# An attention and wave-MLP kernel: new shape of the k and v loads, new order of the first loads, turns by transfers in the last batches, and another planner

## The chip, the cores and the metric

The kernel runs on one core of a Trainium2 chip. The metric is the device time of one execution in microseconds. Five engines work side by side, each through its own list of instructions in order: TensorE (PE, matrix products; PEld is its loading of weights), VectorE (DVE), ScalarE (ACT), GpSimd (POOL) and SyncE (SP, which here only issues transfers). Transfers are issued by SP, ACT or POOL and carried by 16 DMA engines. An instruction that waits holds up all that stand behind it on its engine.

## What is computed

For each of 8 batches, with 576 rows, 8 heads of width 64, and C = 512:

```
kv    = k^T v                      per head (64 x 64)
x     = (q kv) / rms(q kv) * g     heads side by side: 576 x 512
theta = x w_theta
y     = w_tok_r (x cos theta) + w_tok_i (x sin theta)     mixes the 576 rows
u     = x + y
out   = u + max(u w_ch, 0)
```

Inputs are float32, the output is float32; products after kv are done in float16 with float32 sums. The order in which kv sums the 576 rows does not matter to the result beyond rounding.

## The kernel before

Each batch is cut into four full row tiles of 128 rows (tile j holds the rows 4p + j of the first 512) and one tail tile of 64 rows, which is folded into 128 partitions by 256 columns. A batch goes through these steps, whose names are those of the planner:

- load k and v (SP; in batch 0 v by ACT) and q (POOL, which turns float32 into float16 on the way). `load_heads` (L191 to L199) reads four rows per partition, 1 KB, and the 64 last rows as 256-byte pieces into partitions 0 to 63.
- `kv` (L250): 40 products per batch into PSUM; `ko`: copies into the block-diagonal `kbd`.
- q is turned (rows to columns): by PE and a copy in batches 0 and 1 (`qt`, `qo`), by a transposing transfer on SP from batch 2 on (`qd`, L300).
- `raw` (L313, L322): q kv. `sq` (ACT) squares, `ss` (DVE) sums, `rt` (POOL, L351) takes the root, `x` (DVE, L363) multiplies.
- `xt`, `xo`: PE turns x by four transposes a tile (L268) into the PSUM ring `tr` of two, ACT copies the result (L284).
- `th` (L393, L398): x w_theta. `pt` (ACT, L411) and `arg` (DVE, L417) take whole turns off, `abs` (DVE), `sin` (L433) and `cos` (L440) on ACT, `z` (DVE, L453) multiplies by x. The tail tile is moved by four transfers (`zmove`, L461) into `zt`.
- `y` (L476, L480): 9 products a full tile in three parts, with the token weights `wT`. `um` (DVE, L487) adds x. `ut`, `uo`: u is turned as x is. `v` (L393, L398; the same helper): u w_ch. `ug` (POOL, L516) scales u, `fin` (DVE, L526) joins, `st` (SP, L535, L540) stores.

The token weights are loaded once, by POOL, and turned by PE (`wt`, L565, L566: 50 transposes), the copies (`wo`) shared by ACT and DVE. w_theta (L608) lands in the third z buffer and is scaled by DVE (`wth`). w_ch (L611) lands in the buffer of the untransposed token weights, so that its load waits until they have been turned; ACT scales it (`wc`, L552).

The order of all this is not in loops. `add` makes a task for each step, with an engine, a cost and a place in the row; `in_order` (L65) then plays the engines against each other: among the tasks that could start first on an engine it takes the one with the smallest place plus an offset (`OFF`, by kind and phase), and the instructions are recorded in that order. Loads are tasks of a pretended engine "wire" that carries one after another at 3.9 us a megabyte (`MB`). Buffers are rings (`Ring`); `HOP`, `RESHAPE` and `STAY` are costs of going from engine to engine and of changing the shape of PE's products.

Two gates hold transfers back: POOL copies one element of the first v piece before it loads the second half of q, and SP moves one element of the token weights before it loads k and v of batch 1.

Of the kernel before, what the change touches and what calls it, by code (L numbers as in the profile page):

```python
# [17 lines left out]
def off(kind, phase):  # L18
    return OFF.get(kind, (0.0,) * 4)[phase]


# [7 lines left out]
class Task:  # L29


    def __init__(self, kind, eng, cost, fn, deps, pos, takes, tail, shape):
        self.kind, self.eng, self.cost, self.fn, self.deps = kind, eng, cost, fn, deps
        self.phase = 0 if pos < 5 else 1 if pos < 10 else 2 if pos < 35 else 3
        self.key, self.takes, self.tail, self.shape = pos + off(kind, self.phase), takes, tail, shape
        self.readers = []
        self.end = None

OFF = {
    "abs": (-3.7, 3.6, -2.4, -8.5), "arg": (6.9, 12.9, 14.0, 13.4),
    "cos": (13.4, 13.4, 8.2, 7.8), "fin": (14.6, 7.0, 14.8, 13.7),
    "g": (13.0, 13.0, 13.0, 13.0), "hold": (14.0, 14.0, 14.0, 14.0),
    "ko": (11.8, 8.0, 14.0, 13.9), "kv": (13.8, -0.2, 6.1, 7.1), "load": (-5.7, 1.3, 2.9, 2.9),
    "pt": (-7.8, 2.2, -7.1, 3.8), "qd": (11.0, 10.6, 4.6, 4.6), "qo": (-8.0, -2.1, -2.1, -2.1),
    "qt": (4.1, 6.8, 6.8, 6.8), "raw": (-1.7, -7.2, -6.3, -3.9), "rt": (-0.5, 3.8, -5.8, -4.4),
    "sin": (-0.9, 13.7, 7.2, 4.4), "sq": (-1.7, -6.0, -5.7, 1.0), "ss": (-0.6, 4.1, -7.7, 11.0),
    "st": (-7.1, -7.4, -6.6, -8.0), "th": (-1.4, -6.3, 0.6, -1.3),
    "ug": (13.0, 13.9, 12.5, 9.1), "um": (13.8, 13.7, 13.7, 11.8),  # L50
    "uo": (5.2, -4.0, -0.3, -0.7), "ut": (-7.1, 19.0, 15.2, 13.7), "v": (13.7, 12.7, 16.9, 7.7),
    "wc": (-8.0, -8.0, -8.0, -8.0), "wire": (-4.0, -4.8, -4.7, -4.7),
    "wo": (-5.3, -5.3, -5.3, -5.3), "wt": (-1.7, -1.7, -1.7, -1.7),
    "wth": (-4.7, -4.7, -4.7, -4.7), "x": (-8.9, -0.3, -6.7, 5.3),
    "xo": (-7.6, -1.6, -2.9, -1.3), "xt": (-4.2, 7.2, -4.8, 6.1), "y": (13.4, 13.6, 15.3, 14.4),
    "z": (7.4, 4.5, 7.3, 9.7), "zmove": (5.3, 11.7, 6.1, 12.8),
}
HOP = 0.14
SLACK = 0.000
RESHAPE = 0.1  # L60
HEAD = 0.0
STAY = 3.861


def in_order(tasks, spare=(), idle=None):  # L65

    waiting = list(tasks)
    free, shape, order = {}, {}, []  # L70
    while waiting:
        best = {}
        for t in waiting:
            if any(d.end is None for d in t.deps):
                continue
            at = free.get(t.eng, 0.0)
            for d in t.deps:
                at = max(at, d.end + (d.tail + HOP if d.eng != t.eng else 0.0))
            held = [r.held[len(r.held) - r.n] for r in t.takes if len(r.held) >= r.n]
            readers = [x for h in held for x in h.readers]  # L80
            if any(x.end is None for x in readers):
                continue
            for x in readers:
                at = max(at, x.end + (HOP if x.eng != t.eng else 0.0))
            turn = t.shape is not None and shape.get(t.eng, t.shape) != t.shape
            best.setdefault(t.eng, []).append((at, t.key + STAY * turn, t))
        if not best:
            raise ValueError("no task can start")
        picks = []
        for cand in best.values():  # L90
            first = min(c[0] for c in cand)
            picks.append(min(((key, at, i, t) for i, (at, key, t) in enumerate(cand)
                              if at <= first + SLACK), key=lambda c: c[:3]))
        _, at, _, t = min(picks, key=lambda c: (c[1], c[0]))
        was = free.get(t.eng, 0.0)
        n = int((at - was - 0.3) / 0.3) if t.eng == "PE" and was < HEAD else 0
        for r in spare:
            old = r.held[len(r.held) - r.n].readers if len(r.held) >= r.n else []
            if n > 1 and r not in t.takes and all(x.end is not None and x.end + HOP < was for x in old):
                d = Task("idle", "PE", 0.0, lambda r=r, n=n: idle(r, n), [], 0.0, [r], 0.0, None)  # L100
                d.end = was
                r.held.append(d)
                order.append(d)
                break
        t.end = at + t.cost
        if t.shape is not None:
            t.end += RESHAPE * (shape.get(t.eng, t.shape) != t.shape)
            shape[t.eng] = t.shape
        free[t.eng] = t.end
        for r in t.takes:  # L110
            r.held.append(t)
        waiting.remove(t)
        order.append(t)
    return order
# [3 lines left out]
def kernel(  # L118
# [36 lines left out]
    NU, NUT, NX, NXE = 5, 3, 8, 5  # L155
    QD = 2
    UD = 0
    QT_TAIL = 6.0
    UT_TAIL = 6.0
    NKV = 2  # L160
    NZ = 3
# [8 lines left out]
    wnt = const.tile([TL, 2 * S], FP16, name="wnt")  # L170
# [9 lines left out]
    fill = const.tile([P, C], FP16, name="fill")  # L180
# [4 lines left out]
    wch_s = wn[:].rearrange("p j s -> p (j s)")[:, 0:2 * NKC * C].bitcast(FP32).rearrange(  # L185
        "p (kc c) -> p kc c", kc=NKC)
# [4 lines left out]
    def load_heads(eng, dst, src, b, hs):  # L191
        eng.dma_start(
            out=dst[:, hs, 0:NJ, :],
            in_=src[b, hs, 0:SM, :].rearrange("h (p j) d -> p h (j d)", j=NJ),
        )
        eng.dma_start(
            out=dst[0:TL, hs, NJ, :],
            in_=src[b, hs, SM:S, :].rearrange("h s d -> s h d"),
        )  # L199
# [14 lines left out]
    def load_token(w_in, at):  # L214
# [3 lines left out]
        nc.gpsimd.dma_start(out=wnt[:, at:at + S], in_=w_in[SM:S, :])  # L218

    def hold():  # L220

        nc.gpsimd.tensor_copy(out=gate[:], in_=vt[0][0:1, 1, 0, 0:1])

    def hold_next():
# [82 lines left out]
    def raw(b, j):  # L307
        w = C if full(j) else HC
        t = ps.tile([P, w], FP32, tag="raw", bufs=2, name="raw")
# [73 lines left out]
    def x_out(b, j, eng):  # L383
        n = NKC if full(j) else NKC // 2
        d = work.tile([P, n, P], FP16, tag="xT" if full(j) else "xTe", bufs=3, name="xT")
        copy_out(eng, d[:], tr_ps.pop(("x", b, j))[:])
        xT[b, j] = d
# [168 lines left out]
    def w_turn(n):  # L556
        t = ps.tile([P, S], FP16, tag="tr", bufs=2, name="wps")
# [5 lines left out]
        for rows, cols in parts:  # L563
            for jj in range(NJ):
                nc.tensor.transpose(t[rows, jj * P:(jj + 1) * P], wn[:, jj, cols], ident[:])  # L565
            nc.tensor.transpose(t[rows, SM:S], wnt[:, cols], ident[0:TL, 0:TL])  # L566
        tr_ps["w", n] = t

    def w_out(n, eng):
        copy_out(eng, wT[:, n, :], tr_ps.pop(("w", n))[:])  # L570

    def idle(r, n):
        tag = "raw" if r is rings["raw"] else "acc"
        t = ps.tile([P, C], FP32, tag=tag, bufs=r.n, name="idle")
        for _ in range(n):
            nc.tensor.matmul(t[:], ident[:], fill[:], start=True, stop=True)


    tasks = []
    rings = {}  # L580
    def ring(name, n):
        return rings.setdefault(name, Ring(n))

    def add(kind, eng, cost, fn, deps=(), pos=0.0, takes=(), tail=0.0, shape=None):
        t = Task(kind, eng, cost, fn, [d for d in deps if d is not None], pos,
                 [ring(*r) for r in takes], tail + (0.06 if eng == "PE" else 0.0), shape)
        tasks.append(t)
        return t

# [5 lines left out]
    MB = 3.9  # L595
    PS_TR, PS_RAW, PS_ACC = ("tr", 2), ("raw", 2), ("acc", 4)

    def load(queue, cost, mbytes, fn, deps=(), pos=0.0):
        i = add("load", queue, cost, fn, deps, pos)
        return i, add("wire", "wire", mbytes * MB, lambda: None, [i], pos, tail=1.6)  # L600

# [11 lines left out]
    held = None  # L613
    got, q_got, k_got, q_turned = {}, {}, {}, {}
    add("load", "wire", 2.2, lambda: None, [], -99)
    pool = add("load", "POOL", 0.75, lambda: None, [], -99)
    pool, h = load("POOL", 1.0, 0.52, lambda: load_q(0, slice(0, HH)), [pool], -50)
    q_got[0, 0] = [h]
    sp = act = None
    for hp in range(NHP):  # L620
        hs = slice(2 * hp, 2 * hp + 2)
        sp, a = load("SP", 1.2, 0.3, lambda hs=hs: load_heads(nc.sync, kt[0], k, 0, hs),
                     [sp], -49 + hp)
        act, c = load("ACT", 1.2, 0.3, lambda hs=hs: load_heads(nc.scalar, vt[0], v, 0, hs),
                      [act], -49 + hp)
        k_got[0, hp] = [a, c]
        if hp == 0:
            pool = add("hold", "POOL", 0.3, hold, [pool, c], -48)
            pool, h = load("POOL", 1.0, 0.52, lambda: load_q(0, slice(HH, H)), [pool], -47.5)
            q_got[0, 1] = [h]  # L630
            pool, h = load("POOL", 1.3, 0.14, lambda: load_qe(0), [pool], -47.4)
# [241 lines left out]
```

## Time and profile before

| | |
|---|---|
| times of three runs | 229.03, 231.63, 231.85 us (median 231.63) |
| span of the profiled execution | 231.2 us; the time of that execution itself is not given apart from the three, and the median lies 0.43 above the span |
| busy: PE, DVE, ACT, POOL | 201.1, 166.9, 140.6, 125.1 us |
| read from memory, written | 33.10 MB, 9.44 MB |
| share of the 16 DMA engines: hardware queue of SP, software queue of POOL, queue of ACT | 58.7%, 21.5%, 1.7% |
| first kv product, last PE product | 9.96, 226.22 us |

In the profile's rows, "L476 PE MATMUL y<-zm,wT" is line 476, on TensorE, writing y from zm and wT. In the slices each digit is a fortieth of the span (5.8 us) in tenths of business. "PEclk" is the granted clock of TensorE. The busy time of PE counts the whole of each product, which overlap in the pipeline, so a busy PE isn't one at its peak: what a product costs in a row of them is read from the chain.

### The profile page before, as it was taken

To read this page: it belongs to the slowest core of one execution; us is meant where nothing else is said; L and a number is where in the kernel's file an instruction comes from. 1 tells how busy PE (TensorE), PEld (TensorE's weight loads), DVE (VectorE), ACT (ScalarE), POOL (GpSimd) and SP (SyncE) were. 2 spreads that over 40 slices of the span, in tenths; PEclk is the share of its full clock that TensorE was granted. 3 is DMA by queue.
4 is the path that set the end of the run, shared out by engine and by line. 5 is a ranking of instruction groups with operands and counts; after the bars stand their busy time and mean duration, and the time that the engine had idled before them with its cause. 6 is when DMAs were issued, how large, how long until landed. Compare 5 with 4: busy or idle time off the path is not lost.

```text
span 231.2 us, 5222 instructions
## 1 busy us (share of the span) xinstructions
PE 201.1 (87%) x2022; PEld 120.3 (52%) x2022; DVE 166.9 (72%) x314; ACT 140.6 (61%) x285; POOL 125.1 (54%) x117
## 2 busy tenths in 40 slices
PE   0455498997799999999999999999999999998991
PEld 0444345574446555755674666566556755553450
DVE  5126759422699678899987898889879987996451
ACT  2021459433978737986992788388838884784120
POOL 2309590031595097858638880987297339462340
PEclk9999999997999999999999999999999999999999
DMA  5983999996247789999998998899989922102232
GB/s 136 266 223 86 203 283 237 249 293 187 45 146 142 95 234 219 199 245 291 171 124 231 341 202 124 213 278 193 162 241 283 199 70 92 60 14 81 102 123 84
DMA packets 63419, 41.42 MB, mean 179 GB/s; under 512 B 29474, under 2 KB 58274, under 8 KB 63394
## 3 DMA queue, kind: packets, MB, share of 16 engines
q1 hardware_dynamic: 47826, 33.86, 58.7%
q0 software_dynamic: 13904, 6.05, 21.5%
q10 hardware_dynamic: 1664, 1.18, 1.7%
q8 instruction: 16, 0.26, 0.5%
q14 instruction: 9, 0.07, 0.1%
HBM read 33.10 MB, written 9.44 MB: 184 GB/s over the span
## 4 chain that ended last, share of the span: by engine, by line
PE 65%; DVE 9%; ACT 9%; DMA 7%; POOL 4%; issue 4%; SPq 2%; ACTq 0%; DVEq 0%; POOLq 0%
PE y L476 22%; PE th L393 9%; PE v L393 9%; PE kv L250 6%; DMA kt<-in_k_dram 5%; PE xps L268 4%; PE ups L268 3%; POOL rt L351 3%; PE y L480 3%; PE raw L313 2%; PE th L398 2%; ACT pt L411 2%; DVE ss L344 2%; DVE ot L526 2%; PE v L398 1%
## 5 line engine op out<-in xcount | busy, mean ns | idle before, releaser
L351 POOL TENSOR_TENSOR rt<-ss,mhalf 128x8 f32<-128x8 f32 (+1 forms) x40 | 61.6, 1547 | 32.2 <-DVE ss L344 31.9
L516 POOL TENSOR_TENSOR ug<-u,g 128x512 f32<-128x512 f16 (+1 forms) x40 | 42.8, 1077 | 63.4 <-DVE u L487 62.0
L476 PE MATMUL y<-zm,wT 128*128 128x512 f16 x256 | 65.9, 383 | 0.3 <-DVE zm L453 0.3
L476 PEld LDWEIGHTS <-wT 128*128 128x128 f16 x288 | 26.6, 99 | 27.3 <-issue 3.0
L487 DVE TENSOR_TENSOR u<-y,x 128x512 f16<-128x512 f32 (+1 forms) x40 | 25.0, 633 | 15.1 <-PE y L476 12.2
L284 ACT COPY uT<-ups 128x512 f16<-128x512 f16 (+1 forms) x40 | 21.3, 543 | 19.9 <-PE ups L268 19.9
L393 PE MATMUL v<-wch,uT 128*128 128x512 f16 x128 | 32.9, 380 | 0.0
L393 PE MATMUL th<-wth,xT 128*128 128x512 f16 x128 | 32.4, 395 | 0.5 <-ACT xT L284 0.5
L335 ACT ACTIVATE sqb<-raw 128x512 f32<-128x512 f32 x32 | 18.5, 598 | 21.5 <-PE raw L313 21.2
L526 DVE SCALAR_TENSOR_TENSOR ot<-v,ug 128x512 f32<-128x512 f32 (+1 forms) x40 | 25.2, 631 | 8.3 <-PE v L393 2.9
L411 ACT ACTIVATE pt<-th 128x512 f32<-128x512 f32 (+1 forms) x40 | 21.9, 553 | 13.2 <-PE th L393 12.6
L417 DVE SCALAR_TENSOR_TENSOR arg<-pt,th 128x512 f32<-128x512 f32 (+1 forms) x40 | 25.0, 626 | 4.6 <-ACT pt L411 4.3
L440 ACT ACTIVATE sc<-arg,quarter 128x512 f16<-128x512 f32 (+1 forms) x40 | 26.5, 679 | 0.5 <-DVE arg L425 0.4
L344 DVE TENSOR_REDUCE ss<-sqb 128x8 f32<-128x520 f32 x32 | 21.6, 689 | 7.1 <-ACT sqb L335 6.9
L363 DVE TENSOR_TENSOR x<-raw,rt 128x512 f16<-128x512 f32 x32 | 21.9, 683 | 5.0 <-POOL rt L351 4.8
L433 ACT ACTIVATE sc<-arg 128x512 f16<-128x512 f32 (+1 forms) x40 | 23.2, 593 | 1.7 <-DVE arg L417 1.3
L250 PE MATMUL kv<-vt,kt 128*64 128x64 f32 x640 | 23.0, 235 | 1.2 <-DMA vt<-in_v_dram 1.2
L284 ACT COPY xT<-xps 128x512 f16<-128x512 f16 (+1 forms) x40 | 20.5, 547 | 5.5 <-PE xps L268 5.5
L250 PEld LDWEIGHTS kv<-vt,kt 128*64 128x64 f32 x640 | 21.8, 149 | 2.4 <-DMA vt<-in_v_dram 1.6
L453 DVE TENSOR_TENSOR zm<-x,sc 128x1024 f16<-128x1024 f16 x32 | 22.1, 705 | 0.6 <-ACT sc L440 0.5
L284 ACT CAST kbd<-kv 64x256 f16<-64x256 f32 (+1 forms) x30 | 10.5, 352 | 18.9 <-DMA vt<-in_v_dram 11.9
L393 PEld LDWEIGHTS <-xT 128*128 128x128 f16 x128 | 12.1, 100 | 15.0 <-ACT xT L284 2.0
(66 smaller groups left out, 226.8 us busy)
## 6 DMA issues: line engine op xcount, KB each, us to landing
out_dram<-ot SPq DMA_DIRECT2D x32, 256.0 KB, 3.0
kt<-in_k_dram SPq DMA_DIRECT2D x7, 1024.0 KB, 7.1
vt<-in_v_dram SPq DMA_DIRECT2D x7, 1024.0 KB, 10.0
qh<-in_q_dram POOLq DMA_DIRECT2D x7, 512.0 KB, 8.3
kt<-in_k_dram SPq DMA_DIRECT2D x4, 256.0 KB, 6.2
vt<-in_v_dram ACTq DMA_DIRECT2D x4, 256.0 KB, 5.2
zm<-in_moe_w_theta_dram SPq DMA_DIRECT2D x1, 1024.0 KB, 6.5
zt<-zf SPq DMA_DIRECT2D x32, 32.0 KB, 2.1
```

Source lines behind the costliest of these rows:

```text
L250: nc.tensor.matmul(t[i * D:(i + 1) * D, hp - lo, :], kt[b % NKV][:, 2 * hp + i, j, :], vt[b % NKV][:, 2 * hp + i, j, :], start=(j == 0), s ...
L284: nc.scalar.copy(out=dst, in_=src)
L344: nc.vector.reduce_sum(out=ss[:], in_=sq_sb.pop((b, j))[:], axis=AXX)
L351: nc.gpsimd.tensor_tensor(out=rt[:], in0=ss[:], in1=mhalf[:, 0:h], op=ALU.pow)
L393: nc.tensor.matmul(t[:], lhs[:, kc, :], w[:, kc, :], start=first, stop=last)
L411: nc.scalar.activation(out=pt[:], in_=th_ps[b, j][:], func=AFT.Copy, bias=MAGIC)
L417: nc.vector.scalar_tensor_tensor(out=arg[:, 0, :], in0=pt_sb.pop((b, j))[:], scalar=MAGIC, in1=th_ps.pop((b, j))[:], op0=ALU.subtract, op1 ...
L440: nc.scalar.activation(out=sc_sb[b, j][:, 1, :], in_=arg_sb.pop((b, j))[:, 1, :], func=AFT.Sin, bias=quarter[:], scale=-TURN * SHRINK,)
L476: nc.tensor.matmul(t[:], wT[:, w, j * P:(j + 1) * P], r, start=first, stop=last)
L487: nc.vector.tensor_tensor(out=u[:], in0=y_ps.pop((b, j))[:], in1=x_sb.pop((b, j)), op=ALU.add)
L516: nc.gpsimd.tensor_tensor(out=ug[:].rearrange("p (h e) -> p h e", h=h), in0=u_sb[b, j][:].rearrange("p (h e) -> p h e", h=h), in1=g8[:].un ...
L526: nc.vector.scalar_tensor_tensor(out=ot[:], in0=v_ps.pop((b, j))[:], scalar=0.0, in1=ug_sb.pop((b, j))[:], op0=ALU.max, op1=ALU.add,)
```

## The change

1. `load_heads` reads k and v in runs of nine rows: 64 runs a head, of which the first five rows (1280 bytes) go to partitions 0 to 63 and the last four (1024 bytes) to partitions 64 to 127. The sum over rows in kv is the same set in another order. The padding stays where it was.
2. The first loads: SP issues w_theta and g first, then k of batch 0 in three pieces (2, 2 and 4 heads, where there were four of 2); ACT v in the same three pieces; POOL q, both token weights and q of batch 1 with no gate between. The one gate left stands on SP behind k: once the first (imaginary) token weight has landed, w_ch, k and v of batch 1 follow. w_ch now lands in the second z buffer, and its scaling comes before the z of batch 1.
3. x of batches 6 and 7 and u of batch 6 are turned by transposing transfers on SP (`xd`, `ud`) instead of PE and ACT.
4. The token weights' last 64 rows are turned together at the end (`w_turn_last`, 46 transposes in all for 50); two raw tiles of batch 0 go into the PSUM ring `acc` of four instead of `raw` of two.
5. `in_order` follows transfers: at most eight outstanding for SP and ACT together and eight for POOL, queues that share the wire (`Wires`), PE at half speed after idle windows (`Gate`), a delay every 256 PE instructions (`FETCH`), the earliest start first and the place only between equals. Costs and offsets are all new, so the order of every engine changes; the idle products that could be put on PE (`idle`, switched off by `HEAD = 0.0`) are gone.

```diff
     def load_heads(eng, dst, src, b, hs):
-        eng.dma_start(
-            out=dst[:, hs, 0:NJ, :],
-            in_=src[b, hs, 0:SM, :].rearrange("h (p j) d -> p h (j d)", j=NJ),
-        )
-        eng.dma_start(
-            out=dst[0:TL, hs, NJ, :],
-            in_=src[b, hs, SM:S, :].rearrange("h s d -> s h d"),
-        )
+        rows = src[b, hs].rearrange("h (p r) d -> p h (r d)", r=R)
+        eng.dma_start(out=dst[0:TL, hs, 0:LO, :], in_=rows[:, :, 0:LO * D])
+        eng.dma_start(out=dst[TL:P, hs, 0:HI, :], in_=rows[:, :, LO * D:R * D])
...
-    wch_s = wn[:].rearrange("p j s -> p (j s)")[:, 0:2 * NKC * C].bitcast(FP32).rearrange(
-        "p (kc c) -> p kc c", kc=NKC)
+    wch_s = zm[NZ - 2][:].rearrange("p j i c -> p j (i c)").bitcast(FP32)
...
-    def hold():
-
-        nc.gpsimd.tensor_copy(out=gate[:], in_=vt[0][0:1, 1, 0, 0:1])
-
-    def hold_next():
+    def hold():
 
         nc.sync.dma_start(out=gate_s[:], in_=wn[0:1, 0, S:S + 1])
...
+    for a in range(2):
+        q_got[0, a] = [add("lq", "POOL", 0, lambda a=a: load_q(0, slice(HH * a, HH * (a + 1))),
+                           [start], 0, -50 + a, moves=((0.98, 2.05),))]
+    q_got[0, 2] = [add("lq", "POOL", 0, lambda: load_qe(0), [start], 0, -47, moves=(Q_TAIL,) * 2)]
+    for lo, hi in ((0, 2), (2, 4), (4, H)):
+        load_k(0, slice(lo, hi), "SP", (), -50 + lo)
+    got["g"] = add("lg", "SP", 0, load_g, [], 0, -41, moves=((0.4, 0.1), (0.5, 0.1), (0.6, 0.1)))
+    got["wth"] = add("lwth", "SP", 0, load_wth, [], 0, -40, moves=((0.5, 3.2),))
+    for i, w_in, at in ((0, moe_w_tok_i, S), (1, moe_w_tok_r, 0)):
+        got["tok", i] = add("ltok", "POOL", 0, lambda w_in=w_in, at=at: load_token(w_in, at),
+                            [start], 0, -30 + i,
+                            moves=((0.8, 3.7), (0.54, 0.46)))
...
+    held = add("hold", "SP", 0.6, hold, [got["tok", 0]], 0, -38)
...
+    def loads(b):
+        deps = [last.get(("kv", b - NKV)), held]
+        load_k(b, slice(0, H), "SP", deps, NT * (b - 2))
+        load_next_q(b, [*all_of("qt", b - NB), *all_of("rt", b - 2)], NT * (b - 1) - 6.5)
...
+    got["wch"] = add("lwch", "SP", 0, load_wch, [held], 0, -36, moves=((0.5, 3.2),))
...
+    XD, UD = (6, 7), (6,)
...
+            if b in XD:
+                xo = add("xd", "SP", 0, lambda b=b, j=j: x_turn_dma(b, j), x, b, s,
+                         [("xT" + w, NXT)], moves=((1.25 * f, 0.9 * f),))
+                xt = xo
...
+            if b in UD:
+                ut = uo = add("ud", "SP", 0, lambda b=b, j=j: u_turn_dma(b, j), [um], b, s,
+                              [("uT" + w, NUT)], moves=((1.25 * f, 0.9 * f),))
...
+    def x_turn_dma(b, j):
+        n = NKC if full(j) else NKC // 2
+        d = work.tile([P, n, P], FP16, tag="xT" if full(j) else "xTe", bufs=NXT, name="xT")
+        nc.sync.dma_start_transpose(out=d[:], in_=x_sb[b, j])
+        xT[b, j] = d
...
+    def w_turn_last():
+
+        t = ps.tile([P, NT, P], FP16, tag="tr", bufs=2, name="wps")
+        for jj in range(NJ):
+            nc.tensor.transpose(t[:, jj, :], wnt[:, jj:SM:NJ], ident[:])
+        for rows in (slice(0, TL), slice(TL, P)):
+            nc.tensor.transpose(t[rows, NJ, :], wnt[:, SM:S], ident[:])
+        tr_ps["w", "last"] = t
```

The order in which the changed program's engines stand, as far as the prediction uses it: SP: w_theta, g, k of batch 0, the gate, w_ch, k and v of batch 1, v and k of batch 2. PE: q turned, kv of batch 0 first half, two raw tiles, kv second half, two token turns, three raw tiles, three token turns (the last the first that needs the real weights), two x turns, theta of all five tiles with x turns between, then token turns, q turns of batch 1 and the parts of y, kv of batch 1, three raw tiles of batch 1, a part of y that needs zt, two x turns. ACT: squares, a token copy, two x copies, the four scalings of w_ch, the other x copies, then theta's steps.

## The prediction

> **What bounds the kernel now.** First the page's busy shares and slices, then the busy time by stretches, then the chain.
>
> ```profile
> PE 201.1 (87%) x2022; PEld 120.3 (52%) x2022; DVE 166.9 (72%) x314; ACT 140.6 (61%) x285; POOL 125.1 (54%) x117
> ...
> PE   0455498997799999999999999999999999998991
> ```
>
> TensorE (PE) is full from the thirteenth slice (70 us) on; what it loses is lost before. The stretches (start:end, then busy us and instructions of PE, PEld, DVE, ACT, POOL, granted clock, DMA share, GB/s):
>
> ```profile
> 20.00:30.00 10.00, 5.55 (x56) 3.65 (x55) 6.08 (x15) 3.93 (x9) 7.36 (x8) 1.00 0.91 150
> ...
> 50.00:60.00 10.00, 7.35 (x77) 4.91 (x73) 3.55 (x7) 4.75 (x10) 2.31 (x2) 0.83 0.76 196
> 60.00:70.00 10.00, 8.21 (x68) 4.21 (x67) 8.17 (x15) 8.29 (x17) 7.77 (x7) 1.00 0.32 98
> ...
> 140.00:160.00 20.00, 20.00 (x168) 11.38 (x168) 16.83 (x31) 14.09 (x30) 14.40 (x13) 1.00 0.97 204
> ```
>
> The chain that ended last (start, us, what) tells what a matmul costs once PE is fast, and the period:
>
> ```profile
> 9.16 4.29 DMA kt<-in_k_dram
> ...
> 29.32 3.53 PE th L393 x8
> ...
> 47.53 0.73 PE kv L250 x20
> ...
> 51.47 2.23 issue
> 53.97 0.96 PE qps L268 x8
> ...
> 59.46 2.57 ACT wch L552 x4
> ...
> 92.27 2.45 PE kv L250 x80
> ...
> 160.02 2.33 PE kv L250 x80
> ...
> 182.43 2.33 PE kv L250 x80
> ...
> 226.22 0.65 PE v L398 x8
> ```
>
> From kv to kv is 22.4 us. At 29.32 eight theta matmuls take 3.53 us (0.44 each); later eight take 1.73 (0.216). So PE is also at half speed after idle stretches, though the granted clock of that stretch reads 1.00.
>
> I count PE's work in the chain's late rows: 0.2155 us a 512-column matmul, 0.0545 a 256-column one (18 in 0.98), 2.33 a kv, 0.0555 a transpose or a raw matmul (8 in 0.45), 0.03 a 64-column raw one. A batch: y 36 x 0.2155 + 0.98 = 8.74; theta and v 2 x (16 x 0.2155 + 0.44) = 7.78; kv 2.33; raw 1.13; x and u turned, 18 transposes each, 2.00: 21.98. Eight batches 175.8, q turned for two 2.0, token weights 50 x 0.055 = 2.75: **180.5 us**. PE ends at 226.9, 4.3 us before the span, so 46.4 us of PE time are lost. By the program's order, kv of batch 1 (47.53) has 18.2 us of work before it: 29.3 lost. Batch 3 (92.27): 52.6, 39.7 lost. Batch 7 (182.43): 139.4, 43.0 lost; 3.4 more until the end. So a change can win the 39.7 us of the opening, little in the middle, some 3 us in the drain, or take work off PE.
>
> I sum against the profiled span, 231.2 us; the median, 231.63, is 0.43 above it, and I add that for what lies around the span.
>
> **Turns by transfers.** x of batches 6 and 7 and u of batch 6 leave PE: 3 x 18 transposes x 0.0555 = **-3.0 us**. ACT loses 15 copies of some 0.54 us (8.2 us), worth nothing alone, as ACT is 61% busy. The last token turn takes 6 transposes for 10, -0.2. The 15 transfers are issued by SP. The 18 that turn q show 1.2 to 5.8 us of issue (median 1.87) and 3.1 to 9.2 us from issue to landing; an x tile has half the bytes. 15 x 1.87 = 28 us of SP, with queued behind each the stores, whose three buffers hold up the finishing DVE step, then v's PSUM. The share of DMA is 0.19 to 0.40 there, and x of batches 6 and 7 stands well ahead of its theta in the program's order. u is tightest: from the addition that makes the last full u of batch 6 to its v matmul stand 6.7 us of PE work (v 3 x 0.86, y 2 x 1.94, a turn 0.22), against 0.65 + 1.87 + 3.1 = 5.6. Covered by 1 us at the short landing, late by 5 at 9.2. I take 0, since nothing else loads the wires then.
>
> **Runs of nine.** A head of k or v was 128 packets of 1 KB and 64 of 256 B; it becomes 64 of 1280 B and 64 of 1 KB, each kind to one half of the partitions. The trace's packet records have medians of 46 ns (1 KB), 84 (2 KB), 18 (256 B, these into 64 partitions). 1280 B is between 46 x 1.25 = 57 and, at the 256 B rate, 90. Sixteen heads over 16 engines: 128 x 46 + 64 x 18 = 7.0 us before; 64 x 57 + 64 x 46 = 6.6, or 64 x 90 + 64 x 72 = 10.4. So -0.4 to +3.4 us of wire per batch. I take -0.4, 1280 B being nearest to 1 KB. In the full stretch loads hide behind 22 us of PE; only the opening pays. The Trainium skill (SBUF — State Buffer, "Door 1: The DMA port swizzle") says that bandwidth follows how many of the 16 ports the partitions reach, and partitions 0 to 63 reach half of them: by it the sum takes the upper price and comes to 229. Neither packet size goes to half the partitions in bulk here, so the trace can't decide.
>
> **Order of the first loads.** w_theta (1 MB, 32 packets on each engine) goes ahead of k on SP. Beside v's first three transfers (24 packets) and q (64 of 60 ns) it is through at 2.4 + 24 x (84 + 50 + 60) ns + 8 x (84 + 60) ns = 8.2, landed about 9.5 (an estimate of 1.2 us to the landing, zt's shortest being 1.7 with its issue). Eight transfers may be outstanding between SP and ACT, so v's fourth waits for w_theta, and k's third for the g vector behind it. First kv about 11.2 (9.96 before), first half done 15.1 (13.8). The rest of k and v takes turns with q's tail (32 ns) and then the token weights (107): 40 rounds of about 143 ns and 8 of 82 from 10.8, landed about 18.4, as before (18.65), where the last 256 B packets of v waited for their turn to be issued. Then the imaginary token weights land about 22.3, the real ones 26.8, w_channel (behind a gate on the first) 30, k and v of batch 1 40. Before: SP issued w_channel at 47.58, behind four big loads, and ACT scaled it at 59.46.
>
> The step is paid in ACT's queue: w_channel's four scalings now stand ahead of three of the five x copies. ACT waits for 30.0, then 4 x 0.65 (0.73 each before), then copies, theta's rounding, sines (0.64) and cosines (0.72), five token copies: third z at 43.5, fourth 44.8. PE: second-half raws behind two token turns 22.8; x pairs 27.1 and 28.7; theta from 28.4, at half speed; y from 38.7; kv of batch 1 about 46 (47.5 before), with 16.7 us of work done: the same 29.3 lost.
>
> Then batch 1's chain shows: kbd 48.8, square 0.6, sums 0.7, two roots at 1.65, x 0.7: x pair at 54.6, PE waits some 4 us (48.9 to 54.6 less 1.6 of work) and is then slow. It wins on w_channel: the v matmuls, late in 61 to 68 before, fill the gaps. Adding queue by queue I get kv of batch 2 near 67 and of batch 3 near 83.5, with 45.3 us of work done: 38.2 lost, against 39.7.
>
> **Sum.** 177.3 work + 38.2 + 6.7 (what before loses from batch 3 to the end) + 4.3 + 0.43 = 226.9. Taking 1 us off the drain's 3.4, as ACT and DVE have x of the last batches behind them, **226 us**.
>
> **Rivals.**
> 1. *The opening and drain gain more* (222). If zt of batch 0 lands by 50, y and u fill the 4 us wait and PE stays fast. For: batch 1's x comes some 8 us earlier than before (63.9). Against: that y stands behind the third raw of batch 1, which waits for a root. 226 - 4.
> 2. *Half the ports* (229). 64-partition runs go at the 256 B rate: 3.4 us later second half, partly hidden by the other queues. For: no 1 KB packet goes to half the partitions. 226 + 3.
> 3. *Transfers' turns land late* (229). v and theta of the last batches wait for landings of 9 us; the 3.0 us come back as stalls. For: 3.1 to 9.2. Against: idle wires.
> 4. *Slower: token weights behind everything* (233.5). PE is in order, and two token turns stand ahead of the second-half raws, one odd turn (real weights) ahead of the first x turn. If POOL's queue gets a third of the wire until k and v end, the real weights land at 34, not 26.8, and all of the opening moves 7 us: 226 + 7.5. It decides from 27.2, when x is ready, each later us costing one; beyond 32.4 the kernel is slower than before. Against: the rounds above.
> 5. *The planner's order isn't met by the queues* (231): costs written into it for engines differ from the rows (w_channel 0.61 against 0.73, root 1.6 against 1.55); PE, in order, waits in the middle, where before loses 0.8 us a batch. 226 + 5.
>
> **Numbers.** A measurement tells about 2% (4.6 us) from no change. Forecast 0.45, rivals 0.22, 0.08, 0.07, 0.10, 0.08. Faster by over 2% (below 227.0): 0.28 of the forecast's and rival 1: 0.50. Slower by over 2% (above 236.3): part of rival 4 and bad cases of 5: 0.08. Within: 0.42. The range reaches from rival 1 with the drain's whole 3 us on top (219) to rival 4 (234).
>
> **What would show it.** Right: PE transposes down by 58; last PE instruction near 222; w_theta landed before 10.5, w_channel's scalings at 30 to 33; kv of batch 1 at 45 to 47; a PE gap of 3 to 5 us at 49 to 55; no wait on xT or uT from a transfer after 180. Wrong: second kv half after 20; a token turn that waits after 27; theta or v that waits for an SP transfer in the drain; kv period over 23.

## The result

The changed kernel takes **243.69 us** (median of four, 243.06 to 250.3), beside 231.57 us for the kernel before on the same chip: a ratio of 1.054, 95% interval 1.046 to 1.063. It is 5.4% slower where 226.0 us was forecast, and lies outside the range of 219 to 234. The profiled execution has a span of 242.5 us and took 244.24 us. The ratios here and below leave disturbed runs out, so a ratio can lie below the quotient of two medians.

### The profile page after: what moved, and what is told of

Its sections match the earlier page's. It is cut to its first block, busy times and chain, and to the rows that moved or that the text cites. A ratio compares the mean times of both kernels' runs of the same rounds, so it can differ in the third digit from the quotient of the medians.

```text
span 242.5 us, 5111 instructions
## 1 busy us (share of the span) xinstructions
PE 198.9 (82%) x1964; PEld 119.1 (49%) x1964; DVE 170.9 (70%) x316; ACT 133.5 (55%) x270; POOL 127.2 (52%) x116
## 3 DMA queue, kind: packets, MB, share of 16 engines
q1 hardware_dynamic: 47506, 35.63, 66.3%
## 4 chain that ended last, share of the span: by engine, by line
PE 48%; DMA 21%; DVE 16%; ACT 5%; POOL 4%; issue 3%; SPq 2%; POOLq 0%; DVEq 0%
PE y L570 19%; DMA kt<-in_k_dram 9%; PE v L487 9%; PE th L487 6%; PE kv L337 5%; DMA zt<-zf 5%; DMA out_dram<-ot 3%; DMA vt<-in_v_dram 3%; POOL rt L439 3%; DVE arg L511 3%; PE y L574 3%; DVE arg L519 2%; DVE x L451 2%; PE ups L355 2%; DVE ss L432 2%
## 5 line engine op out<-in xcount | busy, mean ns | idle before, releaser
L610 POOL TENSOR_TENSOR ug<-u,g 128x512 f32<-128x512 f16 (+1 forms) x40 | 44.4, 1120 | 46.2 <-DVE ot L620 33.0
L581 DVE TENSOR_TENSOR u<-y,x 128x512 f16<-128x512 f32 (+1 forms) x40 | 25.1, 632 | 13.8 <-PE y L570 8.2
L487 PE MATMUL th<-wth,xT 128*128 128x512 f16 x128 | 34.3, 406 | 0.3 <-ACT xT L371 0.3
L371 ACT COPY uT<-ups 128x512 f16<-128x512 f16 (+1 forms) x35 | 18.4, 544 | 25.6 <-PE ups L355 25.6
L337 PE MATMUL kv<-vt,kt 128*64 128x64 f32 x640 | 24.4, 240 | 8.2 <-DMA vt<-in_v_dram 5.7
L511 DVE SCALAR_TENSOR_TENSOR arg<-pt,th 128x512 f32<-128x512 f32 (+1 forms) x40 | 25.1, 628 | 7.8 <-ACT pt L505 7.7
L337 PEld LDWEIGHTS kv<-vt,kt 128*64 128x64 f32 x640 | 23.1, 153 | 9.9 <-issue 5.2
L371 ACT CAST kbd<-kv 64x256 f16<-64x256 f32 (+1 forms) x30 | 10.5, 351 | 31.0 <-PE kv L337 30.7
L547 DVE TENSOR_TENSOR zm<-x,sc 128x1024 f16<-128x1024 f16 x32 | 23.9, 752 | 1.8 <-ACT sc L534 1.7
L519 DVE TENSOR_SCALAR arg<-arg 128x512 int32<-128x512 int32 (+1 forms) x40 | 19.7, 494 | 0.9
L371 ACT COPY xT<-xps 128x512 f16<-128x512 f16 (+1 forms) x30 | 15.5, 546 | 7.3 <-PE xps L355 7.3
## 6 DMA issues: line engine op xcount, KB each, us to landing
zm<-in_moe_w_ch_dram SPq DMA_DIRECT2D x1, 1024.0 KB, 10.5
```

The lines of the kernel that those rows point to most:

```text
L337: nc.tensor.matmul(t[i * D:(i + 1) * D, hp - lo, :], kt[b % NKV][:, 2 * hp + i, j, :], vt[b % NKV][:, 2 * hp + i, j, :], start=(j == 0), s ...
L371: nc.scalar.copy(out=dst, in_=src)
L487: nc.tensor.matmul(t[:], lhs[:, kc, :], w[:, kc, :], start=first, stop=last)
L511: nc.vector.scalar_tensor_tensor(out=arg[:, 0, :], in0=pt_sb.pop((b, j))[:], scalar=MAGIC, in1=th_ps.pop((b, j))[:], op0=ALU.subtract, op1 ...
L581: nc.vector.tensor_tensor(out=u[:], in0=y_ps.pop((b, j))[:], in1=x_sb.pop((b, j)), op=ALU.add)
L610: nc.gpsimd.tensor_tensor(out=ug[:].rearrange("p (h e) -> p h e", h=h), in0=u_sb[b, j][:].rearrange("p (h e) -> p h e", h=h), in1=g8[:].un ...
```

## The profile after

First the page of the changed kernel: busy time, then the slices of PE and of the DMA engines, then SP's queue (packets, MB, share of 16 engines).

```profile
PE 198.9 (82%) x1964; PEld 119.1 (49%) x1964; DVE 170.9 (70%) x316; ACT 133.5 (55%) x270; POOL 127.2 (52%) x116
...
PE   0035759873899999969999966999999998899993
...
DMA  6999999997999799999779899999652345436524
...
q1 hardware_dynamic: 47506, 35.63, 66.3%
```

PE has 58 instructions less than before, as meant, and 2.2 us less busy time. But the row of nines has two holes, at the eighteenth slice (103 to 109 us) and at the twenty-fourth and twenty-fifth (139 to 152 us), where the kernel before had none. SP's queue carries 5% more bytes (33.86 MB before, the turned tiles come on top) and takes 66.3% of the engines for it, of a longer span, in place of 58.7%. The stretches of the changed kernel (start:end, then length and busy us of PE, PEld, DVE, ACT, POOL, granted clock, DMA share, GB/s) place the holes:

```profile
80.00:100.00 20.00, 19.91 (x245) 12.62 (x243) 17.11 (x33) 15.69 (x34) 16.68 (x15) 1.00 1.11 213
100.00:120.00 20.00, 17.03 (x128) 8.95 (x128) 16.85 (x28) 12.83 (x24) 10.73 (x10) 0.91 1.06 204
120.00:140.00 20.00, 20.00 (x267) 12.80 (x264) 15.17 (x27) 12.75 (x27) 13.21 (x11) 1.00 0.92 164
140.00:160.00 20.00, 15.48 (x188) 10.78 (x188) 13.20 (x25) 12.66 (x29) 10.12 (x9) 0.91 1.17 233
160.00:180.00 20.00, 20.00 (x226) 12.12 (x221) 17.97 (x35) 13.60 (x29) 13.87 (x12) 1.00 0.90 150
```

In both holes the DMA share is over 1 (records of transfers overlap), and the granted clock falls to 0.91. The share alone doesn't make a hole: from 80 to 100 us it is 1.11, and PE is full. The chain that ended last says who was waited for (start, us, what):

```profile
3.52 9.87 DMA kt<-in_k_dram
13.41 11.71 DMA kt<-in_k_dram
25.25 2.42 PE kv L337 x40
...
91.37 8.39 DMA out_dram<-ot
99.78 9.77 DMA zt<-zf
...
111.03 1.71 PE v L487 x4
113.17 1.31 PE th L487 x4
114.48 0.86 PE v L487 x4
...
138.73 8.35 DMA vt<-in_v_dram
147.33 1.82 PE kv L337 x40
```

A move of z's tail tile, 32 KB, is 9.77 us under way; a v lands 8.35 us after its issue and kv stands waiting. Right behind the wait for zt four products of v take 1.71 us, where the next four take 0.86. The list of PE's waits from 40 us on (us in all, times, longest) agrees:

```profile
PE kv L337 <- DMA vt<-in_v_dram: 4.1, 1, 4.1
PE raw L401 <- DVE x L451: 3.7, 1, 3.7
PE y L570 <- DMA zt<-zf: 3.0, 1, 3.0
PE xps L355 <- DVE x L451: 1.1, 1, 1.1
```

By the prediction's way of counting (the start of kv less the PE work ahead of it in the program's order), PE has lost by each point, in us:

| | kv of batch 1 | 2 | 3 | 4 | 7 | PE's end |
|---|---|---|---|---|---|---|
| before | 29.3 | 37.9 | 39.7 | 41.1 | 43.0 | 46.4 |
| forecast for after | 29.3 | | 38.2 | | 41.5 | 43.9 |
| after | 33.0 | 42.7 | 44.0 | 49.6 | 56.9 | 60.9 |

With 177.3 us of work and 4.3 us behind PE's end, 60.9 gives the span of 242.5. The 17.0 us by which after misses the forecast are 5.8 in the opening (to batch 3), 9.6 in the middle (to batch 7) and 1.6 in the drain. The middle is the largest piece, and the one that the prediction held to be safe.

## Experiments

**Theories.** *Half the ports* (P): a load into 64 partitions runs at half the rate, and the transfers of the full stretch, late by it, stall PE. *Opening* (O): the new order of the first loads and the planner lose it. *Turns* (T): transfers' turns on SP hold up the rest.

### e1: the changed kernel with four-row runs

```diff
-        rows = src[b, hs].rearrange("h (p r) d -> p h (r d)", r=R)
-        eng.dma_start(out=dst[0:TL, hs, 0:LO, :], in_=rows[:, :, 0:LO * D])
-        eng.dma_start(out=dst[TL:P, hs, 0:HI, :], in_=rows[:, :, LO * D:R * D])
+        eng.dma_start(
+            out=dst[:, hs, 0:NJ, :],
+            in_=src[b, hs, 0:SM, :].rearrange("h (p j) d -> p h (j d)", j=NJ),
+        )
+        eng.dma_start(
+            out=dst[0:TL, hs, NJ, :],
+            in_=src[b, hs, SM:S, :].rearrange("h s d -> s h d"),
+        )
```

> The changed kernel with the k and v loads of before (four rows of 1 KB on 128 partitions, 64 rows of 256 B); every engine's order stays that of the changed kernel. Theory P (half the partitions at a time: 1280 B and 1 KB packets take 86 and 78 ns, so k and v hold the wires and SP's queue too long): 1 KB packets back at 46 to 58 ns, the waits for zt at 99 to 110 and for v at 143 to 147 (12 us) gone, second half of the first kv 2 to 4 us sooner; 227 to 233 us. Rival O (the order of the first loads and of the engines): within 3 us of the changed kernel, 240 to 244 us.

Measured: 237.28 us, ratio 1.016 [1.007, 1.025], span 232.1 us. The time lies between the two expectations, nearer to P's 227 to 233; 1 KB packets are back at 49 ns and the waits are gone, as P had it, but the second half of the first k and v has landed only 0.2 us sooner (24.9 for 25.1), not 2 to 4. Every engine has the same instructions in the same order as in after, apart from these loads. The stretches of the holes in this run, in the columns of the stretches above:

```profile
100.00:120.00 20.00, 19.32 (x211) 11.24 (x209) 18.28 (x32) 14.37 (x30) 12.86 (x11) 1.00 1.07 202
...
140.00:160.00 20.00, 19.39 (x250) 12.23 (x247) 17.57 (x36) 17.34 (x39) 13.80 (x12) 1.00 1.10 189
```
The holes are gone. PE's waits for zt and for v are gone too; from 40 us on no wait for a transfer is in its list, whose longest rows are these:

```profile
PE raw L406 <- DVE x L456: 3.7, 1, 3.7
PE xps L360 <- DVE x L456: 1.1, 1, 1.1
```

The starts of kv, in us:

| kv of batch | 1 | 2 | 3 | 4 | 5 | 7 | PE's end |
|---|---|---|---|---|---|---|---|
| after (nine rows) | 49.7 | 72.1 | 89.3 | 119.3 | 134.7 | 160.1 | 238.2 |
| e1 (four rows) | 48.2 | 70.6 | 87.9 | 114.2 | 129.6 | 149.7 | 227.8 |
| nine rows cost | 1.5 | 1.5 | 1.4 | 5.1 | 5.1 | 10.4 | 10.4 |

The nine-row runs cost 1.5 us before batch 1, 3.7 between batches 3 and 4 (the wait for zt), 5.3 between batches 5 and 7 (the wait for v) and nothing after the last load. Lined up product by product, the delay against e1 grows by more than the two waits: behind each of them some products run slow (634 ns for 379 behind the wait for zt, 314 for 222 behind the one for v), which costs about 1.5 us each time, and some 1.5 us come back where e1 has short waits of its own. So of the 17.0 us missed, 10.4 are the nine-row runs; 4.4 in the opening, 0.6 in the middle and 1.6 in the drain are not.

### e2: the kernel before with nine-row runs alone

The same edit the other way round, in the old kernel and its old order.

> The kernel before with runs of nine rows alone. Theory P: packets at 80 to 90 ns, a batch of k and v at 11 us of wire for 7 to 8, first kv later by 2 to 4 us and a wait of TensorE for zt or v in the middle; 235 to 242 us. Rival O: 230 to 233 us.

Measured: 245.62 us, ratio 1.063 [1.055, 1.071]. This one part costs 14.4 us by itself, more than the whole change and more than the 235 to 242 expected of P. The opening doesn't lose: kv of batch 1 starts at 46.7 us, 0.8 sooner than before. Kv of batch 4 is 7.3 us late and kv of batch 7 13.3 (195.6 for 182.3), and from there to PE's end both kernels take 44.6 us; the loss is all in the middle, where loads still run. What PE waits for differs with the order: here it is a turned q (4.1 us), not zt.

### e5: the loads alone

Loads of k and nothing else, form by form: full width, lower half, upper half, both halves from two queues, the lower half from two queues, 256-byte pieces. The arithmetic is left out; only the loads are read.

> Loads alone, in phases one after the other: four 1 MB loads of 1 KB packets into 128 partitions; the same k in 1280 B packets into partitions 0 to 63; in 1 KB packets into 64 to 127; both halves at once from two queues; the low half from two queues at once; 256 B packets into partitions 0 to 63. It computes nothing and its output isn't the reference's. Theory P (partitions 0 to 63 share half of the ways in): median packet 46 ns, then 85 to 95, then 70 to 78, then 55 to 65 with both halves (as at full width), then doubled in the sixth phase's neighbour, the low half from two queues: 170 to 190. If it is the packet's size and not the partitions: 1280 B at 57 ns and 1 KB at 46 in the second and third phase.

The DMA rows of this run's page, in slices of 3.4 us (share in tenths, then GB/s):

```profile
DMA  0599906999099907999909997199999999999994
GB/s 0 161 362 350 339 10 152 210 207 193 1 191 207 203 10 159 214 338 345 318 2 210 209 210 132 38 202 222 216 204 227 211 204 226 209 217 214 203 222 90
```

In the slices that lie inside one form, full width (slices 3 to 5) moves 339 to 362 GB/s, the lower half (8 to 10) 193 to 210, the upper half (13 and 14) 203 to 207, both halves at once (18 to 20) 318 to 345, and the lower half from two queues (22 to 24) 209 to 210. The DMA share reads nine tenths and more in all of them: it counts the time in which the engines are held, not what they move.

A 1280-byte packet into partitions 0 to 63 takes 108 ns, a 1 KB packet into 64 to 127 takes 86, against 48 ns for 1 KB at full width (medians). A second queue on the same half brings nothing, and its packets stay at 108 ns, where 170 to 190 were expected; the other half beside it brings the rate of the full width. So it is the partitions written to, not the queue or the packet's size, that sets the rate, and one half has some 0.6 of the full rate. The rule of the Trainium skill (SBUF — State Buffer, "Door 1: The DMA port swizzle"), that 64 neighbouring partitions reach half of the 16 ports, agrees; half of the 436 GB/s that the page gives for all ports would be 218, an estimate just above the measured 203 to 210. The 256-byte packets into 64 partitions, on which the prediction's upper price was built, take 18 ns here as there.

### e11: four-row runs, each load cut into two halves

In e1's kernel the packets, their size, count and places stay; only each transfer of the first 512 rows is cut in two, one for each half of the partitions. A load is thereby three transfers, with the one of the last 64 rows, where e1 and after have two.

```diff
-        eng.dma_start(
-            out=dst[:, hs, 0:NJ, :],
-            in_=src[b, hs, 0:SM, :].rearrange("h (p j) d -> p h (j d)", j=NJ),
-        )
+        lo = src[b, hs, 0:SM, :].rearrange("h (p j) d -> p h (j d)", j=NJ)
+        eng.dma_start(out=dst[0:TL, hs, 0:NJ, :], in_=lo[0:TL])
+        eng.dma_start(out=dst[TL:P, hs, 0:NJ, :], in_=lo[TL:P])
```

> The changed kernel with four-row runs, as in the run that gave 1.016 of the kernel before, but each load of the first 512 rows is cut into two DMAs, one into partitions 0 to 63 and one into 64 to 127. Packets, their size (1024 B), their count and the places they fill stay; only the partitions that one DMA writes at a time are halved. Half-partition theory (the nine-row runs cost because each DMA fills 64 partitions): 1024 B packets of these loads go from 49 ns to 78 to 86 ns, waits for zt and v come back, and the time is 240 to 245, a ratio of 1.04 to 1.06. Rival, the form of the runs (1280 B out of 2304 B strides, or the mapping of rows itself): packets stay near 49 ns and the ratio at 1.01 to 1.025, 233 to 238.

Measured: 247.09 us, ratio 1.067 [1.059, 1.074], a little above the 1.04 to 1.06 expected. The median 1 KB packet of SP's queue goes from 49 ns (e1) to 75. In this run's list of PE's waits, over the whole span, those for zt and v are back, and those for k are longer (2.6 us in e1):

```profile
PE kv L341 <- DMA kt<-in_k_dram: 6.0, 4, 3.7
PE kv L341 <- DMA vt<-in_v_dram: 4.4, 2, 2.4
...
PE y L574 <- DMA zt<-zf: 2.5, 1, 2.5
```

Kv starts at 119.4, 134.7 and 160.6 us for batches 4, 5 and 7, and PE ends at 238.7: after's own numbers within half a microsecond, with no run of nine rows in the kernel. Kv of batch 1 comes at 51.6 us, 2.0 later than in after, which may be the third transfer of each load; but from batch 3 to 7, counted as in the table above, e11 loses 11.5 us and after, with two, 12.9, where e1 loses 3.9. This decides for P: what costs is that a transfer fills one half of the partitions, not the form of the runs.

### e6: four rows in batch 0 only

> The changed kernel with the old row loads in batch 0 alone; batches 1 to 7 keep runs of nine. If most of the loss is in the middle, where zt and v wait behind long loads: 240 to 243 us, kv of batch 1 about 1.5 us sooner than in the changed kernel, the waits at 100 to 110 and 143 to 147 still there. If the opening carries it: 234 to 237 us.

Measured: 246.28 us, ratio 1.061 [1.053, 1.068], no better than after and above both expectations, the one for the middle (240 to 243) being the nearer. Waits for zt (3.3 us) and for the turned q (3.3) remain. The loads of the first batch, which the prediction held to be the only ones that pay, are not where the nine rows cost.

### e9: zt's moves from ACT's queue

Is zt late because its moves stand in SP's queue behind k and v, or because the wires are full? One word is changed: `nc.scalar.dma_start` for `nc.sync.dma_start` in `z_move`.

> The changed kernel, nine-row runs and all, with one edit: the small moves that put zf into zt are issued by ACT's queue and not by SP's, where they stand behind the k and v loads of later batches. In-order theory (the moves are late because they stand behind loads in SP's queue): the 9.8 us from zt's move to its landing in the chain at 99.8 us falls under 3 us, the wait of PE before kv in the stretch from 100 to 110 us goes, and the time falls to 237 to 240. Rival, full wires (the moves share their DMA engines with slowed k and v packets whoever issues them): the landings stay at 4 to 10 us and the time at 242 to 245. Third: the moves land sooner, and the k and v loads, still slow, are late instead: 240 to 243 with waits of kv for vt.

Measured: 261.12 us, ratio 1.124 [1.119, 1.130]; all three expectations missed the time. In the view of the tile zt, the moves of after, from SP, take from issue to landing:

```profile
DMA to landing us min/median/max: 1.8/4.6/12.5
```

and in this run, from ACT:

```profile
DMA to landing us min/median/max: 1.9/5.3/8.3
```

The longest falls from 12.5 to 8.3 us, the median does not fall. PE's wait for zt is gone, but ACT, in order, now stands still for the moves, and 7.1% of the chain is ACT's queue at the line that issues them. In this run's list of ACT's waits:

```profile
ACT kbd L371 <- DMA zt<-zf: 3.3, 1, 3.3
ACT qT L371 <- DMA zt<-zf: 2.5, 1, 2.5
ACT pt L505 <- DMA zt<-zf: 2.2, 1, 2.2
```

So SP's queue doesn't explain the usual 5 us, at most the longest cases; full wires fit it. The run can't price the order by itself, since ACT's stalls cover it.

### The opening: e4 and e7

Both take e1's kernel and put k of batch 0 ahead of w_theta on SP. In e4 DVE's scalings of g and w_theta keep their place; in e7 they move to just before the first theta.

```diff
+        early = [k_got[0, hp][0] for hp in (0, 1, 2)]
+        order = early + [t for t in order if t not in early]
```

and in e7 also

```diff
+        scaled = [t for t in order if t.kind in ("g", "wth")]
+        order = [t for t in order if t not in scaled]
+        at = next(i for i, t in enumerate(order) if t.kind == "th")
+        order[at:at] = scaled
```

> The changed kernel with the old row loads and k of batch 0 ahead of w_theta and g on SP; nothing else is moved. If w_theta ahead of k holds up the first kv: kv of batch 1 2 to 4 us sooner than with the old rows alone, and the time 2 to 4 us less. If the opening hangs on the token weights and POOL's roots: within 1 us of the old rows alone.

> The changed kernel with the old row loads, k of batch 0 ahead of w_theta on SP, and the scalings of g and w_theta on VectorE moved from ahead of the third q copy to just before the first theta. If the opening of the changed kernel is late because k waits for w_theta: first kv at 11 to 13 us for 15.1, second half at 19 to 20 for 23.5, kv of batch 1 at 45 to 46 for 48.2; 231 to 233 us. If token weights or POOL's roots set it: kv of batch 1 within 1 us of 48.2, 234 to 236 us.

Measured: e4 1.036 [1.028, 1.044], worse than e1: the scalings, in DVE's order ahead of a copy of q, now wait for a later w_theta, and PE waits for that copy (its longest wait but one, 8.9 us). e7 1.013 [1.008, 1.019]: first kv at 13.8 us in place of 15.1, second half ready at 22.5 in place of 25.1, but kv of batch 1 only 1.0 us sooner (47.2), and the last PE product at 226.9 for 227.8; that is the second expectation, by which token weights or POOL's roots set the opening. The chain of e7 starts so:

```profile
5.66 18.85 DMA wn<-in_moe_w_tok_r_dram
24.65 1.01 PE wps L666 x8
```

It goes on over the roots and the scaling of w_theta, for which theta waits 1.5 us in its late place. So with k and v sooner the token weights are next, and the two changes of e7 partly cancel. In e7 as in e1 PE then waits 3.7 us for an x of batch 1, behind POOL's roots.

### The turns: e3, e8 and e12

e8 is e1 with the 15 turns given back to PE and ACT, at the same places in the plan. e3 is the kernel before with the turns as transfers, planned anew by its old planner.

> The changed kernel with the old row loads and the 15 turns by transfers given back to TensorE and ScalarE, each at the place where the transfer was issued. If the turns by transfers are worth their 3.0 us of TensorE: 237 to 238.5 us against 234.5. If they come back as waits: 234 to 235.5.

> The kernel before with x of batches 6 and 7 and u of batch 6 turned by transfers, by the old planner. If the 54 transposes' 3.0 us are what it is worth: 228 to 229.5 us, with no wait on xT or uT from a transfer over 1 us. If landings come late in the drain: 231 to 235 us.

Measured: e8 242.87 us, 1.047 [1.042, 1.052], beyond the 237 to 238.5 expected. Beside e1's 1.016 the transfers save 3.1% (7 us) in the new order, of which 3.0 us is the work. Where the other 4 arise is not shown: e8 turns on PE and ACT at the places that were planned for transfers, and a wait there for x would be a loss of the place and not of the turn. e3 1.071 [1.061, 1.082], outside both of its expectations: the old planner, given other costs, orders the last batches anew, and theta waits 4.7 us for a turned x. It says nothing on the turns alone. e12 therefore keeps every other instruction of the old order and swaps in the transfers for x of batches 6 and 7, in the kernel of e10 (below).

```diff
+    def x_made(b, j):
+        x_make(b, j)
+        if b in XD and (j % 2 or not full(j)):
+            for jj in (j - 1, j) if full(j) else (j,):
+                x_turn_dma(b, jj)
```

> The kernel before with the channel weights early (0.988 of the kernel before when alone), and the x of batches 6 and 7 transposed by transfers from SP, issued as soon as x is made, into k's first buffer, which is idle by then; the tasks keep their places in the plan, so no other instruction moves. 72 transposes of PE and 10 copies of ACT go. Theory (PE bounds the drain, and a transfer that starts where x is made lands before theta needs it): 72 x 0.026 = 1.9 us of PE and the turns' waits go, 225 to 228, a ratio of 0.97 to 0.983. Rival (theta waits for transfers that land 3 us and more after their issue, or SP's queue holds q's turns of batch 7 behind them): 229 to 233, waits of th for the turned x in the stretch after 160 us.

Measured: 243.07 us, ratio 1.050 [1.043, 1.057]; the theory missed, and the rival's mechanism came, at far more than its price (229 to 233). The first row of PE's waits in this run:

```profile
PE th L408 <- DMA kt<-x: 12.0, 7, 8.1
```

and SP's timeline around the longest of them (start, us, what):

```profile
168.31 1.61 SPq L550 DMA_DIRECT2D out_dram<-ot  x1
170.03 3.11 SPq L299 DMA_TRANSPOSE qD<-qh  x1
173.25 2.51 SPq L385 DMA_TRANSPOSE kt<-x  x2
```

A turned x of batch 6 (in k's idle buffer) lands 2.3 to 3.4 us after its issue. But this x is made by 166.9 us, and SP comes to it only at 173.25, behind a load of v, a store (which waits 1.4 us for DVE) and q's turn of batch 7; theta, which starts at 176.73, has been due since 168.6. The turn is cheap; its place in SP's order is not.

### e10: w_channel early, in the kernel before

```diff
-    wch_s = wn[:].rearrange("p j s -> p (j s)")[:, 0:2 * NKC * C].bitcast(FP32).rearrange(
-        "p (kc c) -> p kc c", kc=NKC)
+    wch_s = zm[NZ - 2][:].rearrange("p j i c -> p j (i c)").bitcast(FP32)
...
-        _, g = load("SP", 0.5, 1.05, load_wch, [t1, sp], -36)
+        sp, g = load("SP", 0.5, 1.05, load_wch, [sp], -36)
...
-                    [co, *all_of("y", b - NZ)], s, [] if full(j) else [("zf", 2)])
+                    [co, *all_of("y", b - NZ), *(channel_ready if b == NZ - 2 else ())], s,
+                    [] if full(j) else [("zf", 2)])
```

> The kernel before, four-row runs, with one edit: the channel weights land earlier, in the second z buffer, behind v of batch 1 and ahead of k and v of batch 2; the first z of batch 1 then waits until they are scaled. It asks whether the opening can gain from loads' order alone, without the rest of the change. Theory (the channel weights' landing at about 59 us stands on the chain of the opening): 2 to 4 us less, 227 to 230. Rival (the roots and token weights bound the opening whatever the channel weights do): within 1 us of the kernel before, 230 to 232. Other side: k of batch 2 is pushed back by the 2.5 us of the weights and kv starts later: 232 to 234.

Measured: **229.57 us** (six runs), ratio 0.988 [0.984, 0.992]: 1.2% faster than the kernel before and faster than every other kernel here. Its chain, to be read against that of before in the prediction, where the scaling of w_ch starts at 59.46:

```profile
38.97 6.06 DMA zt<-zf
...
48.76 1.90 PE kv L249 x60
50.66 0.98 PE y L479 x18
55.72 2.57 ACT wch L551 x4
...
69.30 2.33 PE kv L249 x80
```

w_ch is issued at 31.67 us, before k and v of batch 2, instead of 47.58. ACT scales it 3.7 us sooner, and kv of batch 2 starts at 69.1 instead of 72.9. PE's order is the same, and 3.5 to 4.5 us stay won from there to PE's end (223.4 for 226.8). The theory held: the order of a few loads is worth this much by itself.

## Why the prediction was wrong

**The step that failed** is "Runs of nine", with its sentence "In the full stretch loads hide behind 22 us of PE; only the opening pays". Two things were wrong in it.

1. *The wire.* It took -0.4 us a batch, "1280 B being nearest to 1 KB". The median packets in after are 86 ns (1280 B) and 78 ns (1 KB), where 57 and 46 were taken: 16 x 64 x (86 + 78) / 16 ns = 10.5 us a batch for 7.0, the other end of the bounds (+3.4). (In e5, with no other queue beside them, they are 108 and 86.) The nearest row by bytes was not the nearest by partitions: the only packets that went to one half were the 256-byte ones, and they were set aside. The rate that rival 2 took was right, at a chance of 0.08.
2. *The cover.* Rival 2 still priced it at 3 us, paid once. The cover named was PE's 22 us a batch; but what k and v share is the wires, and the last line of the stretches that the prediction shows (140 to 160 us) gives them a DMA share of 0.97. So 3.5 us more a batch were not hidden and fell on whatever was needed next: zt (3.0 us of PE's wait), v (4.1). These 7.1 us of waits stand beside 9.0 us lost in the middle against e1; the other 1.9 us are what is left of the slow products behind the two waits (some 3 us, in stretches whose granted clock is 0.91 where e1's reads 1.00) after e1's own short waits. The sentence named the wrong place too: e2 loses nothing in the opening and 13.3 us behind it.

**Order of the first loads** failed as well, and with four-row runs it is the larger part of what is left. The change was forecast to win 1.5 us by batch 3; in e1 it loses 2.9 there (42.6 against 39.7), 4.4 of the 17.0. Its links came late one by one: the first kv at 17.3 us (11.2 forecast), the second half landed at 25.1 (18.4), w_ch scaled from 34.8 (30.0), kv of batch 1 at 49.7 (46). With four-row runs the second half still lands at 24.9 and kv of batch 1 comes at 48.2, so only 1.5 us of it is the half ports. w_theta was not late: its 1 MB is through by 6 us, where 8.2 was forecast. Late is the issue of k behind it. From SP's list of waits in after:

```profile
SPq L289 <- DMA vt<-in_v_dram: 6.1, 1, 6.1
```

The prediction held k's third transfer back for the g vector. SP stood already at the second, until an earlier transfer of v had landed, issued it at 10.55 us and saw it land at 17.2, just ahead of the first kv. When the rounds of packets were to begin, at 10.8, SP was still issuing the last five of k's six transfers (10.55 to 13.41), and the last of them took 11.7 us to land beside q and the token weights.

**Batch 1's chain** held up: a wait of PE of some 4 us for x was forecast, and one of 3.7 us is in the list, from 54.5 us.

**Turns by transfers**: 3.0 us of PE work did go (54 of the 58 instructions), at no wait: no transfer-turned x or u is in after's list of waits, so rival 3 did not come. e8 makes the turns worth more than forecast in this order, if its places are fair; e3 and e12 make them cost in the old one.

**Rival 1** (222) did not come: the opening lost. **Rival 4** (token weights behind everything) did not decide: the token turns stand behind kv of the second half and ran without a long wait; it was the second half itself that was late. **Rival 5** (an order that the queues don't meet, 231) comes near what remains with four-row runs, 1.016, but not by its waits in the middle: from batch 3 to 7 e1 loses 3.9 us where before loses 3.3, and the rest is the opening's.

**The drain** gave 4.0 us lost where 3.4 less 1.0 was forecast; in e1, without the half ports, it is 4.0 as well. That ACT and DVE have less to do there brought nothing.

## What to carry to other kernels

Price a load by the partitions that it fills before its packet size: the two halves of k and v, one behind the other, take half as long again as the loads of four rows (10.5 us for 7.0), whatever the runs look like. Side by side from two queues the two halves moved as much as the full width in e5; no kernel here tries that. Before calling a transfer hidden, read the DMA share of the stretch, not the business of the compute engine: at 0.97 to 1.17 in the middle of the kernel before, 3.5 us more a batch were not hidden, and the next transfer in line, large or small, came late for them. A share near 1 is a warning and no more: in e5 it reads the same at 207 GB/s and at 350. And where engines and queues run in order, a move that is cheap by itself (z's moves on ACT, x's turn on SP) costs what its place behind other waits costs; of this change, the one part that gained in the old kernel is to start an early weight load before a queue of large ones.

## What the runs showed of the hardware

- Half the partitions: 193 to 210 GB/s from one or two queues, 318 to 345 with both halves from two queues at once, 339 to 362 at full width (e5); 1 KB packets 48 ns at full width, 86 into the upper half alone, 1280 B 108 ns into the lower.
- The DMA share reads nine tenths in both cases (e5): it doesn't tell a half-width load from a full one.
- A small transfer among full wires: 32 KB moves land 2.1 us after their issue in the median before (6.6 at worst), 3.5 in e1 and 4.6 in after (12.5 at worst), and another queue does not make the median shorter (5.3). Half-width loads in the old order (e2) leave it at 2.2, with 8.1 at worst, so the order of the program has a part in it.
